# Local and summary attention with a gated network: work units of 384 tokens in place of 512

## The chip, the cores and the metric

The kernel runs on one core of one Trainium2 chip. The metric is device time in microseconds (us) from the first to the last instruction of that core. A few names for the engines, as the profile uses them: PE is the matrix engine (its weight loads are listed apart as PEld), DVE the vector engine, ACT the scalar engine, POOL the GpSimd engine, SP the engine whose queue starts nearly all DMA transfers. PE reads operands from SBUF and writes to PSUM; the kernel holds PSUM tiles of 128 partitions by 512 float32 values.

## The reference

Inputs are q, k and v of shape (batch 4, heads 8, sequence 768, head size 64) and four weight matrices. Each query sees the 31 keys nearest to it and, besides, one summary key for each block of 32 keys of its batch (24 summaries); the network then runs over all 3072 tokens.

```python
k_sum = k.reshape(B, H, nb, block, D).max(axis=3)     # block 32, nb 24
v_sum = v.reshape(B, H, nb, block, D).mean(axis=3)
scores_l = scale * q @ k.T, masked to |i - j| < 16
scores_s = scale * q @ k_sum.T + log(block)
a = softmax over [scores_l, scores_s] together
x = (a @ [v, v_sum]), heads side by side              # 3072 x 512
out = (((x @ w1) * (x @ w2)) @ w3) @ w_out            # w1, w2: 512 x 1024; w3: 1024 x 1024; w_out: 1024 x 512
```

## The kernel before

**Products.** The network is computed with each operand split in two parts of 32-bit "fp32r" form, a high one and a low one, so each product is three matmuls (L113): high by high, low by high, high by low. w3 and w_out are multiplied once, at the start, into one matrix `wp` ("the fold", 192 matmuls of 512 columns). The weights come as 64-bit words of 1 MB a tile, and each tile is turned into its high and low part on the chip: ACT L164, DVE L173 and L176, ACT L190 (high part), DVE L109 (low part, tile `w`).

**Units and steps.** All 3072 tokens are one row of 24 blocks of 128 tokens; a batch is 6 blocks. The row is cut into units of `TOKENS` tokens, and a unit has four attention steps, one for each pair of heads. `NBLK` is the number of blocks in a unit, `NU` the number of units, `NS` the number of steps. A step loads its q, k and v (L306, L308, L291), puts in the summaries of its batch (POOL L318 for keys, L298 for values; `batches(u)` makes one copy for each batch that the unit touches), computes scores (PE `sc`, L331), mask and minimum (DVE L345), exponential and sum (ACT L359, one instruction for each block and head), the scaling (L364, L365, L368 or its kin), transposes (PE `tp`, L388), two copies out of PSUM (`pt`, L393 on ACT and L397 on DVE), the product with v (PE `po`, L408), and the split into `x` (ACT L419, DVE L109).

**The network of a unit.** `gate` makes, for each of 8 slices f, two sums over four x tiles: w1 into one PSUM tile, w2 into the next, 12 matmuls each and `U` columns wide (U is TOKENS). ACT copies the first out (`g`, L448), DVE multiplies it with the second (L453), ACT and DVE split the result into `h` (L454, L109). `project` then makes, for each block, one sum of 24 matmuls of 512 columns with `wp` (ACT L472 copies it out, and a DMA from ACT's queue stores it). Both take turns on the same two PSUM tiles, named `mm`.

**What sets the order.** PE, SP (and, in parts, ACT, DVE, POOL) follow the order in which the program is written; where they don't, a scheduler orders by priority. The network's matmuls are one stream, dealt out by a count of columns. In the start, a table of ticks (`LOADS`, `WORK`, `FIRST`) says when loads, conversions and the first eight steps begin; the stream may then go as far as `TO_SLOTS`. In it the summaries of the second batch are prepared as well. After it, a loop takes two steps at a time: transposes of the last two, scores of the next two, outputs of the last two, and then half a unit of the stream:

```python
NU = B * S // U
NS = NU * NPAIR                       # NPAIR = 4
NFIRST = 2 * NPAIR                    # steps of the start: two units
UNIT = 3 * (2 * U * NC * NF + DO * NF * NBLK)
TO_SLOTS = ALL_FOLD + 0.96 * UNIT
run(ALL_FOLD + UNIT * (1 + (n / m if n <= m else 1 + (n - m) / NPAIR)))
```

The summaries of the third and fourth batch are prepared in the start's loop or in later turns of the loop (`coming`, `turns`), by how many steps there are before a batch is needed.

Of the kernel before, what the change touches and what calls it, by code (L numbers as in the profile page):

```python
# [23 lines left out]
LOC = P + 2 * PAD  # L24
CUT = 96
BIG = -8.0e9
TOKENS = 512
PIECE = 1024
AHEAD = 2

# [40 lines left out]
def attention_moe(ctx, tc, qG, kW, kT, vP, vW, vB, mask, w1, w2, w3T, wo, out):  # L71
# [3 lines left out]
    NB = S // BLOCK  # L75
    U = TOKENS
    NBLK = U // P
# [784 lines left out]
```

## Time and profile before

| | |
|---|---|
| median of 2 runs | 533.62 us (533.4 to 533.84) |
| the profiled execution: its span, from the first to the last instruction, the one time its page gives | 533.5 us |
| PE busy / weight loads busy | 511.2 us (96%) / 421.4 us (79%) |
| DVE / ACT / POOL busy | 240.6 / 225.4 / 95.9 us |
| matmuls of the gates (128x512) | 1152, of the projection 576, of the fold 192 |
| DMA | 68.78 MB, mean 129 GB/s |

The page lists busy time by engine, then the span in 40 slices with the granted clock of PE, then the chain of work that ended last, followed back from the last instruction, and groups of like instructions with their busy time, the mean of one and the idle time before them. PE's matmuls overlap one another, so the mean of one is longer than the distance from one start to the next; distances are read from rows of the timeline that hold several matmuls. A "busy" window in the start can also hold matmuls that wait.

### The profile page before, as it was taken

Reading aid. Unit: us, or ns where it says so; the run is one execution under the profiler, and the core shown is the slowest. Engines: PE = TensorE matmul, PEld = TensorE weight load, DVE = VectorE, ACT = ScalarE, POOL = GpSimd, SP = SyncE. Lnnn points to the kernel's source line nnn. Section 1 sums busy time; section 2 is a strip of 40 time slices with the busy share of each in tenths; the row PEclk is TensorE's granted clock in tenths of the full one; section 3 lists DMA queues with packets and bytes.
Section 4 is the critical chain, followed back from the end, with each engine's and each line's share of the span. In section 5 each row is a group of like instructions: output and inputs, shape, how many; then the busy total and the mean of one; then the engine's idle time right before and its main releaser. Section 6 shows DMA issues by size and latency. Waiting matters only on the chain.

```text
span 533.5 us, 9766 instructions
## 1 busy us (share of the span) xinstructions
PE 511.2 (96%) x3888; PEld 421.4 (79%) x3888; DVE 240.6 (45%) x667; ACT 225.4 (42%) x627; POOL 95.9 (18%) x158
## 2 busy tenths in 40 slices
PE   1889989999999999999999999999999999999997
PEld 0667767888888888888888888888888888888885
DVE  5889987798534326435244043251042350222210
ACT  5587964674626226135154063361172361222210
POOL 2020635001033202305005014014023031000000
PEclk9989997999999999999999999999999999999999
DMA  8995699804834013453040150050150011100001
GB/s 346 413 411 220 252 325 413 316 2 139 274 131 167 0 55 122 151 172 134 0 177 1 60 195 1 1 177 20 49 187 2 14 69 40 39 3 0 1 20 59
DMA packets 21166, 68.78 MB, mean 129 GB/s; under 512 B 2304, under 2 KB 2432, under 8 KB 18560
## 3 DMA queue, kind: packets, MB, share of 16 engines
q1 hardware_dynamic: 17664, 61.86, 31.6%
q10 hardware_dynamic: 3456, 6.29, 3.1%
q8 instruction: 30, 0.49, 0.4%
q14 instruction: 16, 0.13, 0.1%
HBM read 61.85 MB, written 6.29 MB: 128 GB/s over the span
## 4 chain that ended last, share of the span: by engine, by line
PE 87%; DMA 5%; DVE 4%; ACT 2%; issue 1%; POOL 0%; SPq 0%; POOLq 0%; ACTq 0%
PE mm L113 76%; PE po L408 4%; PE sc L331 4%; DMA rows<-in_vP_dram 2%; PE tp L388 2%; DVE wf L176 2%; DMA wraw<-in_w_dram 1%; DVE w L109 1%; DMA wraw<-in_wo_dram 1%; ACT sm L359 1%; DVE wf L173 1%; ACT wf L164 1%; DVE sm L345 0%; ACT w L190 0%; DVE ks L236 0%
## 5 line engine op out<-in xcount | busy, mean ns | idle before, releaser
L113 PE MATMUL mm<-x,w 128*128 128x512 f32 x1152 | 264.3, 391 | 0.0
L113 PEld LDWEIGHTS mm<-x,w 128*128 128x128 f32 x1152 | 216.5, 188 | 45.3
L113 PE MATMUL mm<-wp,h 128*128 128x512 f32 x576 | 133.3, 390 | 0.0
L113 PEld LDWEIGHTS mm<-wp,h 128*128 128x128 f32 x576 | 107.7, 188 | 22.6
L359 ACT ACTIVATE sm<-sm,mx 128x120 f32<-128x120 f32 x192 | 73.6, 385 | 16.3 <-DVE mx L345 16.3
L453 DVE TENSOR_TENSOR g<-mm,g 128x512 f32<-128x512 f32 x48 | 33.1, 690 | 88.7 <-PE mm L113 85.4
L454 ACT CAST h<-g 128x512 fp32r<-128x512 f32 x48 | 29.5, 618 | 90.6 <-DVE g L453 90.6
L113 PE MATMUL mm<-w,w 128*128 128x512 f32 x192 | 51.2, 419 | 14.8 <-ACT w L190 12.0
L113 PEld LDWEIGHTS mm<-w,w 128*128 128x128 f32 x192 | 37.3, 200 | 25.7 <-ACT w L190 12.7
L364 POOL TENSOR_SCALAR mx<-mx 128x8 f32<-128x8 f32 x24 | 6.8, 283 | 275.5 <-ACT sm L359 275.3
L472 ACT COPY o<-mm 128x512 f32<-128x512 f32 x24 | 14.0, 584 | 82.5 <-PE mm L113 82.5
L397 DVE COPY pt<-tp 120x512 f32<-120x512 f32 x22 | 14.3, 684 | 75.2 <-PE tp L388 75.2
L109 DVE TENSOR_TENSOR h<-g,h 128x512 fp32r<-128x512 f32 x48 | 35.2, 736 | 25.6 <-ACT h L454 25.4
L448 ACT COPY g<-mm 128x512 f32<-128x512 f32 x48 | 28.1, 586 | 39.0 <-PE mm L113 38.4
L298 POOL COPY v<-vs 24x512 f32<-24x512 f32 (+1 forms) x64 | 40.7, 635 | 8.9 <-DMA v<-in_vW_dram 5.9
L345 DVE CUSTOM_DVE_ANT_0 sm<-sc,mask_sb 128x120 f32<-128x120 f32 x192 | 41.1, 274 | 0.0
L359 ACT ACTIVATION_READ_ACCUMULATOR sm<-sm,mx 128x1 f32 x192 | 36.2, 188 | 0.0
L368 POOL TENSOR_TENSOR sm<-sm,mx 128x960 f32<-128x960 f32 x16 | 28.7, 1793 | 5.6 <-DVE mx L365 5.6
L109 DVE TENSOR_TENSOR x<-po,x 128x512 fp32r<-128x512 f32 x24 | 16.6, 690 | 28.6 <-ACT x L419 28.5
L190 ACT CAST w<-wf 128x1024 fp32r<-128x1024 f32 (+1 forms) x22 | 21.3, 968 | 17.3 <-DVE wf L176 17.2
L408 PEld LDWEIGHTS po<-pt,v 120*64 120x64 f32 x768 | 24.5, 141 | 4.0 <-issue 2.5
L408 PE MATMUL po<-pt,v 120*64 120x64 f32 x768 | 26.6, 228 | 0.9 <-POOL v L298 0.5
(35 smaller groups left out, 287.9 us busy)
## 6 DMA issues: line engine op xcount, KB each, us to landing
v<-in_vW_dram SPq DMA_DIRECT2D x24, 512.0 KB, 6.4
wraw<-in_w3T_dram SPq DMA_DIRECT2D x8, 1024.0 KB, 13.0
wraw<-in_w_dram SPq DMA_DIRECT2D x8, 1024.0 KB, 9.3
k<-in_kW_dram SPq DMA_DIRECT2D x20, 368.0 KB, 5.3
raw<-in_kT_dram SPq DMA_DIRECT2D x16, 392.0 KB, 3.7
q<-in_qG_dram SPq DMA_DIRECT2D x24, 256.0 KB, 4.9
raw<-in_vB_dram SPq DMA_DIRECT2D x12, 512.0 KB, 3.8
out_dram<-o ACTq DMA_DIRECT2D x24, 256.0 KB, 2.0
```

Source lines behind the costliest of these rows:

```text
L109: eng.tensor_tensor(dst, src, hi.bitcast(F32), ALU.subtract)
L113: nc.tensor.matmul(acc, lhsT=a, rhs=b, start=first and i == 0, stop=last and i == len(terms) - 1)
L190: nc.scalar.copy(t[:, 0, some], f[:, some])
L298: nc.gpsimd.tensor_copy(v[at : at + NB, g, blocks], src.unsqueeze(1).broadcast_to([NB, n, P]))
L331: nc.tensor.matmul(sc[h][64 * g : 64 * g + 64, i * KR : (i + 1) * KR], lhsT=q[rows, i * P + 64 * g : i * P + 64 * g + 64], rhs=k[rows, i, ...
L345: nc.vector.tensor_tensor_reduce(out=sm[:, j], in0=sc[h][:, i * KR : (i + 1) * KR], in1=mask_sb[:, 0 if blk == 0 else 2 if blk == BLOCKS - ...
L359: nc.scalar.activation(sm[:, j], sm[:, j], AF.Exp, bias=mx[:, 0, j : j + 1], scale=-1.0, accum_out=mx[:, 1, j : j + 1])
L368: nc.gpsimd.tensor_tensor(sm, sm, mx[:, 2].unsqueeze(2).broadcast_to([P, NI, KR]), ALU.mult)
L408: nc.tensor.matmul(po[cols, at : at + 64], lhsT=v[:KR, g, i, cols], rhs=pt[g][:, (h * NBLK + i) * 64 : (h * NBLK + i + 1) * 64], start=Tru ...
L448: nc.scalar.copy(g, a[:, :U])
L453: nc.vector.tensor_tensor(g, acc[1][:, :U], g, ALU.mult)
L454: nc.scalar.copy(h[:, 0], g)
```

## The change

One constant is changed. `TOKENS` goes from 512 to 384, and with it `U` from 512 to 384, `NBLK` from 4 to 3, `NU` from 6 to 8 and `NS` from 24 to 32. A batch of 768 tokens is then exactly two units. With 512, the second and fifth units held two blocks of one batch and two of the next, and their eight steps took the summaries of two batches.

```diff
-TOKENS = 512
+TOKENS = 384
```

What follows from it: the gates have 1536 matmuls of 384 columns in place of 1152 of 512. The projection has 576 of 512 columns as before. The attention's PE instructions are the same in number in all, 12 a step for `sc`, `tp` and `po` in place of 16, but the loop runs 13 times in place of 9. The eight steps of the start now cover the first batch alone. Copies of a PSUM tile (`pt`, `x`, `g`, `h`) are 384 wide, and there is a third more of them; `UNIT` and `TO_SLOTS` shrink with the unit. The host lays out q, k and v in the narrower units. The third batch's summaries are now prepared by turns of the loop, as the fourth's were.

PE, from the last scores before the first gates to the fourth gate sum, before (tiles with a number are weights; `x16` in the list counts an instruction with its like):

```order
L388 MATMUL tp<-ident,sm 120x64 x16
L331 MATMUL sc<-k,q 64x120 x32
L408 MATMUL po<-pt,v 64x64 x16
L113 MATMUL mm<-x,w_827 128x512 x12
L113 MATMUL mm<-x,w_857 128x512 x12
```

and after the change:

```order
L388 MATMUL tp<-ident,sm 120x64 x12
L331 MATMUL sc<-k,q 64x120 x24
L408 MATMUL po<-pt,v 64x64 x12
L113 MATMUL mm<-x,w_768 128x384 x12
L113 MATMUL mm<-x,w_797 128x384 x12
```

Nothing changes place here: the attention work is three quarters in number, and the gate sums are as many but narrower.

DVE, in the middle of the first unit's gates, where the last weight tiles are converted (`g` is the gate product L453, `h` and `w12` are the low parts L109; w12_902 is the third w1 tile, w12_919 the third w2 tile), before:

```order
L109 TENSOR_TENSOR w12_902<-wf_893,w12_902 128x1024
L173 TENSOR_SCALAR wf_910<-wf_910 128x1024
L109 TENSOR_TENSOR h_1086<-g_1065,h_1086 128x512
L109 TENSOR_TENSOR h_1086<-g_1116,h_1086 128x512
L109 TENSOR_TENSOR h_1173<-g_1158,h_1173 128x512
L176 SCALAR_TENSOR_TENSOR wf_910<-wraw_885,wf_910 128x1024
L173 TENSOR_SCALAR wf_921<-wf_921 128x1024
L453 TENSOR_TENSOR g_1190<-mm_1192,g_1190 128x512
L109 TENSOR_TENSOR w12_919<-wf_910,w12_919 128x1024
```

and after the change (w12_842 and w12_856 are those two tiles, `ISA` is L345's minimum):

```order
L109 TENSOR_TENSOR w12_842<-wf_833,w12_842 128x1024
L173 TENSOR_SCALAR wf_848<-wf_848 128x1024
L109 TENSOR_TENSOR h_996<-g_976,h_996 128x384
L109 TENSOR_TENSOR h_996<-g_1023,h_996 128x384
L109 TENSOR_TENSOR h_1077<-g_1062,h_1077 128x384
L453 TENSOR_TENSOR g_1094<-mm_1096,g_1094 128x384
L176 SCALAR_TENSOR_TENSOR wf_848<-wraw_825,wf_848 128x1024
L109 TENSOR_TENSOR h_1077<-g_1094,h_1077 128x384
L173 TENSOR_SCALAR wf_858<-wf_858 128x1024
L345 ISA sm_905,mx_906<-sc_907,mask_sb_65 128x120
L345 ISA mx_906 128x1
L109 TENSOR_TENSOR w12_856<-wf_848,w12_856 128x1024
```

The fourth gate product (g_1190 before, g_1094 now) stood behind the L176 of the third w2 tile and stands ahead of it now, and one `h` and one L345 more stand between that L176 and the tile's low part.

## The prediction

> **What bounds the kernel now.** I read the page's engine row first, then the chain of waits, then windows and the timeline of PE.
>
> ```profile
> PE 511.2 (96%) x3888; PEld 421.4 (79%) x3888; DVE 240.6 (45%) x667; ACT 225.4 (42%) x627; POOL 95.9 (18%) x158
> PE   1889989999999999999999999999999999999997
> 382.99 1.09 PE tp L388 x32
> 384.08 1.98 PE sc L331 x64
> 386.06 2.02 PE po L408 x64
> 388.08 32.86 PE mm L113 x144
> 420.94 1.09 PE tp L388 x32
> 529.98 0.02 issue
> 530.00 0.59 ACT o L472
> ```
>
> PE is full from about the fifth slice. Later the chain is on PE alone: rounds of `tp`, `sc`, `po` and 144 matmuls, with nothing late between them; one round takes 420.94 - 382.99 = 37.95 us. The window of that part and the one before it, and the first gates:
>
> ```profile
> 0.00:85.19 85.19, 66.81 (x625) 51.17 (x625) 70.61 (x145) 58.37 (x134) 21.85 (x41) 0.95 0.86 333
> 85.19:529.98 444.79, 444.44 (x3266) 370.18 (x3264) 169.98 (x522) 166.49 (x492) 74.03 (x117) 1.00 0.26 90
> 85.19 44.72 PE L113 MATMUL mm<-x,w 128*128 128x512 f32 x192
> ```
>
> (Columns: time, then busy time of PE, PEld, DVE, ACT, POOL, the clock, the DMA share, GB/s.) In the start DVE is busy 70.6 of 85.2 us and the DMA engines 86%; from 85.19 PE is busy 444.4 of 444.8 us. So the time is: **when the gates begin (85.19) + the PE work behind that (444.8) + the end (3.5)** = 533.5, the profiled span, 0.1 us under the median of the runs, 533.62. What matters is what the change does to each, and which new waits PE meets.
>
> **Cost of a gate matmul.** Both widths stream the same columns in all (1152 x 512 = 1536 x 384). The question is the toll of one matmul.
>
> ```profile
> 35.96:38.52 2.56, 2.56 (x8) 0.50 0.98 404
> 35.96 3.19 PE L113 MATMUL mm<-w,w 128*128 128x512 f32 x7
> 287.21 5.15 PE L113 MATMUL mm<-wp,h 128*128 128x512 f32 x22
> L113 PE MATMUL mm<-x,w 128*128 128x512 f32 x1152 | 264.3, 391 | 0.0
> L113 PEld LDWEIGHTS mm<-x,w 128*128 128x128 f32 x1152 | 216.5, 188 | 45.3
> ```
>
> In the second row 7 matmuls at half clock (0.50) begin within 2.56 us, 0.427 us apart, which is 0.2134 at full clock if all of it scales. At full clock (third row) 22 last 5.15 us; less one length of 0.39 that is 4.76 / 21 = 0.2266 apart. So 0.0132 us a matmul is not streaming. If it is paid once a matmul, 384 columns take 0.75 x 0.2134 + 0.0132 = 0.1733; if it grows with the columns, 0.1700. Gates before: 1152 x 0.2266 = 261.0. After: 1536 x 0.1733 = **266.2 (+5.2)**, or 261.1 (0). I take the toll per matmul: a cost that grew with the columns would be expected at half clock too, and there is none to see. The other end stays in the range. [...] The projection keeps 576 x 0.2266 = 130.5.
>
> **Cost of the rounds.** A round's attention part is 37.95 - 144 x 0.2266 = 5.32 us. What of it shrinks with the unit is seen by setting one step against two:
>
> ```profile
> 66.91 0.68 PE L388 MATMUL tp<-ident,sm 64*120 64x64 f32 x16
> 67.53 1.05 PE L331 MATMUL sc<-k,q 64*64 64x120 f32 x32
> 68.51 1.67 PE L113 MATMUL mm<-w,w 128*128 128x512 f32 x6
> 70.11 1.15 PE L408 MATMUL po<-pt,v 120*64 120x64 f32 x32
> 71.19 1.20 PE L113 MATMUL mm<-w,w 128*128 128x512 f32 x4
> ```
>
> One step of `tp`, `sc`, `po` takes 0.62, 0.98, 1.08 us to the next row's start, two take 1.09, 1.98, 2.02. So 0.15 + 0.14 us are fixed, and 5.32 - 5.09 = 0.23 more is the way in and out of the network's matmuls: 0.5 us a round. The rest times 0.75 gives 4.1; I take 4.15, with 4.0 and 4.35 as ends (nothing fixed; some of `sc` fixed too). Behind the first gates there were 10 such rounds (one in the start, nine of the loop, the last without `sc`): 53.2 - 2.0 = 51.2. Now 14: 58.1 - 1.5 = **56.6**. Four rounds more cost about 2 us, and the rest of the difference is work moved behind the first gates, since the eight early steps cover 768 tokens and no longer 1024.
>
> Sum behind the first gates, before: 261.0 + 130.5 + 51.2 = 442.7, and 444.8 measured, so 2.1 are small waits and a cold clock, which I keep. After: 266.2 + 130.5 + 56.6 + 2.1 = **455.4**.
>
> **When the gates begin.** The last step before them, and what held it:
>
> ```profile
> 44.45 0.68 PE L388 MATMUL tp<-ident,sm 64*120 64x64 f32 x16
> 60.30 0.61 POOL v L298
> 61.64 1.03 PE po L408 x28
> 68.66 0.33 SPq L306
> 69.52 7.58 DMA wraw<-in_w_dram
> 82.27 1.08 PE L331 MATMUL sc<-k,q 64*64 64x120 f32 x16 [1.03 <-POOL k L318]
> v<-in_vW_dram SPq DMA_DIRECT2D x24, 512.0 KB, 6.4
> q<-in_qG_dram SPq DMA_DIRECT2D x24, 256.0 KB, 4.9
> ```
>
> The load of the first w2 tile stands in SP's queue behind a q load (68.66) that waits for the fourth pair's scores on PE (67.53). From 44.45 us PE comes there with three `tp`, two `sc`, two `po`, some 6 us; a quarter less is 1.5. The POOL copies of value sums that held `po` (60.30) are a quarter narrower, some 0.7; the first three q and the first v, a quarter smaller, are 0.32 MB less at the 404 GB/s quoted above, 0.8 us. So that load starts about 3 us earlier. Then DVE has a quarter less of minima and copies in the fourth pair, and the wait of 1.03 us on the second batch's key summaries goes, since no early step touches that batch. I take 4 us in all: **81.2**. Ends: 79.5, and 85.2 if DMA or DVE, full as they are, give nothing back.
>
> **A new wait in the first unit.** There the last six weight tiles are converted while the gates run, and DVE does both in one order. Its durations, and the returns from ACT:
>
> ```profile
> L109 DVE TENSOR_TENSOR w<-wf,w 128x1024 fp32r<-128x1024 f32 x18 | 22.4, 1248 | 5.0 <-ACT w L190 5.0
> L176 DVE SCALAR_TENSOR_TENSOR wf<-wraw,wf 128x1024 uint32<-128x1024 uint32 x18 | 22.4, 1242 | 0.2
> L173 DVE TENSOR_SCALAR wf<-wf 128x1024 uint32<-128x1024 uint32 x18 | 13.8, 769 | 3.4 <-ACT wf L164 3.4
> L453 DVE TENSOR_TENSOR g<-mm,g 128x512 f32<-128x512 f32 x48 | 33.1, 690 | 88.7 <-PE mm L113 85.4 <-ACT sm L359 1.6 <-ACT wf L164 1.3
> L236 DVE TENSOR_REDUCE ks<-raw 128x24 f32<-128x768 f32 x16 | 14.9, 943 | 5.3 <-DMA raw<-in_kT_dram 5.3
> 88.87 1.23 DVE L109 TENSOR_TENSOR w<-wf,w 128x1024 fp32r<-128x1024 f32 x1 [1.12 <-ACT w L190]
> 97.37 0.69 DVE L453 TENSOR_TENSOR g<-mm,g 128x512 f32<-128x512 f32 x1 [1.18 <-PE mm L113]
> 109.30 1.23 DVE L109 TENSOR_TENSOR w<-wf,w 128x1024 fp32r<-128x1024 f32 x1
> 116.86 1.22 DVE L109 TENSOR_TENSOR w<-wf,w 128x1024 fp32r<-128x1024 f32 x1
> ```
>
> Before, the third w2 tile was done at 110.5 (third row from the end, plus its length) and wanted at 85.2 + 0.8 (cold clock) + 108 x 0.2266 = 110.5, behind nine sums of 12: no reserve. Now PE wants it 0.8 + 108 x 0.1733 = 19.5 us behind the first gate. DVE has until then, from the fourth pair's `pt` on, by the order: 5 L173, 4 L176, 4 L109 of weights, 9 gate or x operations (0.55 each, by 0.68 at 512 and 1.25 at 1024 columns), 2 L236: 20.7 us, and two returns from ACT of 1.1: 22.9. It begins some 0.9 us before the first gate (the copy of `pt`, then `po`), so the tile is done about 22 us behind it. **PE waits 2.5 us**; 0 if DVE waits for nothing else, since then the returns are covered, 9 in the second rival. The table of ticks and the weights' bytes are unchanged, so narrower gates aren't fed faster.
>
> **What is hidden.** A third more PSUM copies on ACT and DVE: the gates give them 12 x 0.1733 = 2.08 us a sum in place of 2.72. The L453 row shows 85.4 us of waiting on PE, so DVE had been early nearly every time. In a round, ACT must get its copy of a sum in between exponentials before 2.08 us are over; by the order at most five stand ahead of one, and they begin before the sum ends. At 0.3 us a loop round, were this wrong, it would cost 13 x 0.3 = 4 us. The POOL copies for straddling steps (eight of 256 columns became four of 384) lie beside PE's matmuls. The end, 3.5 us, is unchanged: the projection and its last store are the same.
>
> **Sum.** 81.2 + 455.4 + 2.5 + 3.5 = 542.6; I say **542.5 us**, 1.7% slower. About 2% (10.7 us, so 544.3 and 522.9) is what the measurement tells from no change.
>
> **The rivals.**
> 1. *The toll isn't per matmul.* Gates take 261 us, then the sum is 537.4; with no toll at all at 384 columns (1536 x 0.160 = 245.8) 522. For it: I have one width only at full clock. Against: half clock shows none. Chance 18%. [...]
> 2. *Weights come no sooner* (clearly slower): start bound by DMA and conversion, the last w2 tile ready at 118.1 as before (last row above). The gates then end at 118.1 + 36 x 0.1733 = 124.3 in place of 81.2 + 0.8 + 33.3 = 115.3; that wait of 9 us for 2.5 makes 549. It decides over 2% from a tile 2 us later than in my sum. For it: DVE 83% busy in the start. Against: four q and four v a quarter smaller, 0.8 MB less to load. 16%.
> 3. *Copies late in the rounds*, 4 us as above: 546.5. Against: no PE wait in the loop before. 6%.
> 4. *The weight load sets the pace.* If a load of 0.188 us had the array to itself, matmuls couldn't come closer than 0.19: 1536 x 0.19 = 292, the sum 568. Against it, two loads begun in 0.30 us:
>
> ```profile
> 16.81 0.30 PEld L113 LDWEIGHTS mm<-w,w 128*128 128x128 f32 x2 [0.68 <-ACT w L190]
> ```
>
> so the second started 0.11 behind the first, and 0.11 is under 0.17. [...] 4%.
>
> My own case has 56%, range 537 to 547, a fifth of it above 544.3.
>
> **Chances.** Slower by over 2%: 11 of my case, 15 of the second rival, 5 of the third, 4 of the fourth, 35%; faster by over 2%: 2% (the far end of the first rival); within: 63%. The range 534 to 549 leaves out the weight-load case, half of the second rival and the far end of the first, under 2 in 10.
>
> **What would show it.** Right: gate matmuls 0.173 apart; a loop round of 29.0 us (96 x 0.1733 + 36 x 0.2266 + 4.15); first gate near 81; one PE wait of 2 to 3 us on a `w` tile in the first unit, none in the loop. Wrong: 0.170 or 0.162 or 0.19 apart (rivals 1 and 4), rounds over 29.3 with waits on L448 or L453 (rival 3), the first unit's gates ending more than 39 us behind their start (rival 2).

## The result, and the profile after

The kernel with units of 384 takes 552.78 us in the median of two runs (551.33 to 554.22), 1.0369 times the kernel before (95% interval 1.0291 to 1.0447): slower. The forecast was 542.5 with a range to 549. The profiled execution has a span of 552.4 us, 18.9 more than before's. Medians and ratios in this document leave out three executions that ran far slower than the others of the same kernel (645 us and more).

The page of the changed kernel: the engine row, PE in 40 slices, and the clock granted to PE.

```profile
PE 523.6 (95%) x4272; PEld 475.0 (86%) x4272; DVE 247.3 (45%) x723; ACT 230.7 (42%) x671; POOL 99.3 (18%) x174
PE   1988978899999999999999999999999999999997
PEclk9998997989999999999999999999999999999999
```

PE is busy 12.4 us longer, and the clock row dips in the fourth, seventh and ninth slices, in the start and in the first unit. The chain of waits in the loop (start, length, what):

```profile
204.14 0.85 PE tp L388 x24
205.00 1.63 PE sc L331 x48
206.62 1.55 PE po L408 x48
208.17 25.01 PE mm L113 x141
233.18 0.85 PE tp L388 x24
```

A round is 233.18 - 204.14 = 29.04 us, all on PE, as 37.95 was before. The loop is what was forecast, so the miss lies ahead of it. The span in three windows: to the first gate, the first unit's gates, and the rest (columns as in the prediction: time, busy PE, PEld, DVE, ACT, POOL, clock, DMA share, GB/s):

```profile
0.00:86.11 86.11, 63.45 (x529) 47.99 (x529) 67.89 (x130) 53.52 (x114) 20.61 (x39) 0.97 0.82 321
86.11:126.08 39.97, 37.64 (x194) 37.06 (x193) 29.68 (x61) 23.09 (x51) 5.12 (x9) 0.90 0.42 166
126.08:548.50 422.42, 422.04 (x3552) 389.95 (x3552) 149.72 (x533) 153.49 (x505) 73.53 (x126) 1.00 0.25 82
```

The first gate comes at 86.11 where 81.2 was forecast. The 192 gate matmuls behind it take 39.97 us where 33.3 would do, at a mean clock of 0.90. From 126.08 on PE waits for 0.4 us in all. The timeline of PE across the first two windows shows what it waited for (idle time and releaser in brackets):

```profile
84.84 1.33 PE L408 MATMUL po<-pt,v 120*64 120x64 f32 x20 [4.24 <-DVE pt L397]
86.11 21.09 PE L113 MATMUL mm<-x,w 128*128 128x384 f32 x108
108.71 0.44 PE L113 MATMUL mm<-x,w 128*128 128x384 f32 x1 [1.51 <-ACT w L190]
109.97 16.27 PE L113 MATMUL mm<-x,w 128*128 128x384 f32 x83 [0.82 <-DVE w L109]
```

The wait on the third w2 tile (1.51 + 0.82 us) was forecast; the 4.24 us on the copy `pt` of the fourth step were not. DVE's timeline ahead of that copy:

```profile
75.09 0.14 DVE L254 TENSOR_SCALAR vs<-vs 128x32 f32<-128x32 f32 x1
79.35 0.85 DVE L173 TENSOR_SCALAR wf<-wf 128x1024 uint32<-128x1024 uint32 x1 [4.12 <-ACT wf L164]
80.23 1.41 DVE L176 SCALAR_TENSOR_TENSOR wf<-wraw,wf 128x1024 uint32<-128x1024 uint32 x1
81.56 0.68 DVE L109 TENSOR_TENSOR wp<-mm,wp 128x512 fp32r<-128x512 f32 x1
82.16 0.94 DVE L236 TENSOR_REDUCE ks<-raw 128x24 f32<-128x768 f32 x1
83.02 1.21 DVE L109 TENSOR_TENSOR w<-wf,w 128x1024 fp32r<-128x1024 f32 x1
84.16 0.54 DVE L397 COPY pt<-tp 120x384 f32<-120x384 f32 x1
```

DVE stands idle for 4.12 us until the first w2 tile has landed and ACT has begun on it; `pt` waits in DVE's order behind three operations on that tile, a low part of `wp` (L109) and a reduction of the second batch (L236). SP's queue shows that this tile's load (`wraw`) was issued no earlier than before, where it was 69.52:

```profile
66.25 0.33 SPq L246 DMA_DIRECT2D raw<-in_vB_dram  x1
67.92 0.33 SPq L231 DMA_DIRECT2D raw<-in_kT_dram  x1
69.19 0.33 SPq L306 DMA_DIRECT2D q<-in_qG_dram  x1
69.57 0.42 SPq L308 DMA_DIRECT2D k<-in_kW_dram  x1
70.04 0.42 SPq L144 DMA_DIRECT2D wraw<-in_w_dram  x1
```

### The profile page after: what moved, and what is told of

Read it like the earlier page. It is cut to its first block, busy times and chain, and to the rows that moved or that the text cites. A ratio compares the mean times of both kernels' runs of the same rounds, so it can differ in the third digit from the quotient of the medians.

```text
span 552.4 us, 10758 instructions
## 1 busy us (share of the span) xinstructions
PE 523.6 (95%) x4272; PEld 475.0 (86%) x4272; DVE 247.3 (45%) x723; ACT 230.7 (42%) x671; POOL 99.3 (18%) x174
## 4 chain that ended last, share of the span: by engine, by line
PE 86%; DMA 4%; DVE 4%; ACT 3%; POOL 1%; issue 1%; SPq 0%; POOLq 0%; ACTq 0%
PE mm L113 75%; PE po L408 4%; PE sc L331 4%; PE tp L388 2%; DMA rows<-in_vP_dram 2%; DMA wraw<-in_w_dram 1%; DVE wf L176 1%; DVE w L109 1%; DMA wraw<-in_wo_dram 1%; ACT wf L164 1%; DVE wf L173 1%; DVE ks L236 1%; DVE wp L109 1%; POOL v L298 1%; ACT sm L359 1%
## 5 line engine op out<-in xcount | busy, mean ns | idle before, releaser
L113 PE MATMUL mm<-x,w 128*128 128x384 f32 x1536 | 273.7, 338 | 2.3 <-ACT w L190 1.5
L113 PEld LDWEIGHTS mm<-x,w 128*128 128x128 f32 x1536 | 269.9, 190 | 4.0 <-ACT w L190 1.8
L454 ACT CAST h<-g 128x384 fp32r<-128x384 f32 x64 | 32.4, 509 | 90.5 <-DVE g L453 90.5
L453 DVE TENSOR_TENSOR g<-mm,g 128x384 f32<-128x384 f32 x64 | 35.6, 556 | 70.5 <-PE mm L113 67.9
L397 DVE COPY pt<-tp 120x384 f32<-120x384 f32 x30 | 15.4, 551 | 94.5 <-PE tp L388 94.5
L109 DVE TENSOR_TENSOR h<-g,h 128x384 fp32r<-128x384 f32 x64 | 38.7, 607 | 26.0 <-ACT h L454 25.2
L448 ACT COPY g<-mm 128x384 f32<-128x384 f32 x64 | 30.4, 475 | 37.4 <-PE mm L113 36.6
L345 DVE CUSTOM_DVE_ANT_0 sm<-sc,mask_sb 128x120 f32<-128x120 f32 x192 | 42.5, 274 | 0.6 <-PE sc L331 0.6
L298 POOL COPY v<-vs 24x384 f32<-24x384 f32 x64 | 37.8, 590 | 13.0 <-DMA v<-in_vW_dram 9.9
L368 POOL TENSOR_TENSOR sm<-sm,mx 128x720 f32<-128x720 f32 x24 | 33.4, 1391 | 7.6 <-DVE mx L365 7.6
L109 DVE TENSOR_TENSOR x<-po,x 128x384 fp32r<-128x384 f32 x32 | 17.8, 557 | 32.4 <-ACT x L419 30.5
```

The source lines that it names most:

```text
L109: eng.tensor_tensor(dst, src, hi.bitcast(F32), ALU.subtract)
L113: nc.tensor.matmul(acc, lhsT=a, rhs=b, start=first and i == 0, stop=last and i == len(terms) - 1)
L298: nc.gpsimd.tensor_copy(v[at : at + NB, g, blocks], src.unsqueeze(1).broadcast_to([NB, n, P]))
L345: nc.vector.tensor_tensor_reduce(out=sm[:, j], in0=sc[h][:, i * KR : (i + 1) * KR], in1=mask_sb[:, 0 if blk == 0 else 2 if blk == BLOCKS - ...
L368: nc.gpsimd.tensor_tensor(sm, sm, mx[:, 2].unsqueeze(2).broadcast_to([P, NI, KR]), ALU.mult)
L397: nc.vector.tensor_copy(pt[1], tp[1][:KR, :U])
```

## The experiments

All times are medians of repeated runs beside runs of the kernel before, whose medians in these comparisons lie between 532.26 and 532.58 us. "First gate" is the start of the first gate matmul in the profiled execution, "gates' end" the end of the first unit's gates (before: 85.19 and 129.74; after the change: 86.11 and 126.08). These marks come from one execution each and shift with the half clock that fell into it (some 3.7 us in the first unit of the changed kernel), so the medians decide.

### The toll of a matmul

**Two halves (units of 512).** Each gate matmul of 512 columns is split in two of 256; nothing else changes.

```diff
-  products(a[:, :U], [(t[:, 0, c, fs], x[c][:, 0]), ...], c == 0, c == NC - 1)
+  for half in (slice(0, U // 2), slice(U // 2, U)):
+      products(a[:, half], [(t[:, 0, c, fs], x[c][:, 0, half]), ...], ...)
```

> Units of 512 as before, but every gate matmul is issued as two of 256 columns (2304 in place of 1152, the same columns in all). If each matmul pays a fixed 13.2 ns besides its columns, they come 0.1067 + 0.0132 = 0.120 us apart, gates take 276 us in place of 261, and the time is 547 to 550 us. If the toll grows with the columns, 0.1133 apart and no change (533 to 535 us). If the weight load's own time counts as well (two loads begun 0.107 us apart), nothing is added, since 0.107 is under 0.120.

Measured: 548.22 us, ratio 1.0295 (1.0264 to 1.0327), 15.6 us more for 1152 more matmuls: 13.5 ns each. Gate matmuls start 0.120 us apart at 256 columns, 0.173 at 384, 0.2266 at 512. The three lie on a line, 0.0533 per 128 columns plus 0.0133. The toll is paid per matmul, as forecast. Each matmul here has a weight load of its own (2304 of each), so the runs don't tell whether it belongs to the matmul or to the pair.

**No straddling (units of 512).** Steps whose unit holds blocks of two batches take the summaries of the first batch for all of them, so the attention computed there is not the one asked for, but the copies for two batches are gone.

```diff
-            if at < to:
-                yield b, slice(at, to), to - at
+            if at == 0 and to > 0:
+                yield b, slice(0, NBLK), NBLK
```

> Units of 512 as before, but the steps that straddle two batches take the summaries of the first of the two for all their blocks (so their output isn't the attention asked for): one copy in place of two, and no wait for the second batch in the fifth to eighth step. This is the straddling's price alone, without narrower units. If it is as small as the wait it causes on PE in the profile (1.03 us at 82.27), 532 to 533.6 us. Rival: straddling holds the start more than the profile shows, and the time falls by over 4 us.

Measured: 532.04 us, ratio 0.9994 (0.9981 to 1.0006). Straddling cost nothing that the medians show, so its removal had nothing to give.

### What holds the first gate and the first unit

**Copy first (384).** The `pt` copies of the first four steps get priority in DVE's and ACT's order.

```diff
-  pt = evacuate(transposes(...), SECOND[s])
+  tps = transposes(...)
+  with tc.high_priority(offset=SOONER):
+      pt = evacuate(tps, SECOND[s])
```

> Units of 384, and in the first four steps the copies of the transposes out of PSUM (pt) get the priority that the gates' copies have; on DVE the fourth step's copy then stands ahead of the low part of the first w2 tile, but still behind that tile's L173 and L176. Theory 'order on DVE': PE's wait of 4.24 us on that copy comes from what stands ahead of it on DVE; without the low part (1.2 us) and a key summary (0.9) the first gate comes 2 us sooner, and the half-clock spell behind the wait covers less: 549 to 550 us. Rival 'late tile': both hang on the load of the first w2 tile (issued at 70.04, landed at 78.08), so the first gate stays within 1 us of 86.1 and the time within 1 us of 552.8.

Measured: 553.36 us, ratio 1.0396 (1.0370 to 1.0422). The first gate came 2.6 us earlier, at 83.51, and the gates ended later, at 127.75, with waits of 0.8, 3.6 and 1.1 us on weight tiles. An earlier first gate is worth nothing here, since the tiles behind it came no earlier.

**Second batch later (384).** Since no early step touches the second batch any more, its loads and reductions can move from ticks 17 to 33 to ticks 48 to 58, and what needs them behind that.

```diff
-  17: [lambda: load_second(2), lambda: fetch_sums(0)],
-  21: [lambda: load_second(0), lambda: load_second(1), lambda: fetch(5), ...],
...
+  48: [lambda: load_second(0), lambda: load_second(1)],
+  50: [lambda: second_batch(0), lambda: load_second(2)],
...
```

> Units of 384, and the preparation of the second batch's summaries (four loads of 512 KB, four of 392 KB, eight reductions on DVE of 0.95 to 1.2 us) is moved from the start to behind the first gates, since no step before the ninth needs it. Theory 'volume': the start is held by the work that DVE and DMA do for the second batch; before the first gate about 2.5 MB (6 us at 400 GB/s) and 6 us of DVE go, the first gate comes 4 to 6 us sooner, the tile waits in the first unit go, 543 to 546 us. Rival 'late tile': the load of the first w2 tile waits behind a q load for the fourth step's scores on PE, whatever DVE does; the first gate moves by 1 to 2 us, 550 to 551.5 us.

Measured: 548.72 us, ratio 1.0300 (1.0267 to 1.0333). First gate at 81.63, gates' end at 121.88: a good 4 us gained, between the two theories' numbers.

**Load first (384).** Only the q and k loads of the fifth step move by one tick, behind the first w2 tile's load in SP's queue; the second batch stays where the change left it.

```diff
-  22: [..., lambda: first_keys(3), lambda: fetch(4), lambda: fill(3), ...],
-  23: [lambda: second_batch(1)],
+  22: [..., lambda: first_keys(3), lambda: fill(3), ...],
+  23: [lambda: fetch(4), lambda: second_batch(1)],
```

> Units of 384, the second batch where the change left it; the first w2 tile's load stands ahead of the q load that waits for PE's scores, but still behind two loads of the second batch. Theory 'that q load': the tile lands up to 2 us earlier, the first gate at 82 to 84, 549 to 551 us. Rival 'the second batch's loads and reductions are the other half': its loads wait for their buffers until DVE has reduced what was there, so the queue is held all the same, the first gate stays at 85 to 86 and the time at 551.5 to 553 us.

Measured: 553.14 us, ratio 1.0389 (1.0350 to 1.0427): no gain, though the first gate came at 81.07, just where the forecast had it, and earlier than either theory said. PE's timeline tells why:

```profile
81.07 18.48 PE L113 MATMUL mm<-x,w 128*128 128x384 f32 x96
100.08 0.44 PE L113 MATMUL mm<-x,w 128*128 128x384 f32 x1 [0.53 <-ACT w L190]
101.47 2.18 PE L113 MATMUL mm<-x,w 128*128 128x384 f32 x11 [0.95 <-DVE w L109]
106.20 0.69 PE L113 MATMUL mm<-x,w 128*128 128x384 f32 x1 [2.54 <-ACT w L190]
108.16 16.68 PE L113 MATMUL mm<-x,w 128*128 128x384 f32 x83 [1.27 <-DVE w L109]
```

Of the 5 us gained by the first gate all but 1.4 are lost again by the gates' end (124.68), in four waits on two tiles, 5.3 us, and in the half clock around them (mean clock 0.88 from 81.07 to 124.68).

**Both (384).** The second batch later and the load first.

> The second batch's loads and reductions come at ticks 48 to 58 as in the run that moved them alone (548.72 us, first gate at 81.63), and the q load that stood ahead of the first w2 tile's load in SP's queue stands behind it. Theory 'order of SP's queue': the load of that tile no longer waits for PE's scores, so the first gate begins at 77 to 80 and the following tiles come sooner by the same; the first unit's gates still last about 40 us; 544 to 547 us. Rival 'conversion': DVE and ACT convert the tiles of the first unit no faster, so what the first gate gains goes into waits of PE on w tiles; the first unit's gates last 42 to 44 us; 548 to 549 us.

Measured: 544.22 us, ratio 1.0210 (1.0172 to 1.0249), 8.6 us under the changed kernel. The profiled execution is the quickest of the four (542.04). Its windows and its PE timeline:

```profile
0.00:79.51 79.51, 60.72 (x528) 45.93 (x528) 63.57 (x121) 54.89 (x116) 19.36 (x41) 1.00 0.78 304
79.51:114.01 34.50, 33.69 (x197) 33.37 (x193) 29.87 (x63) 21.41 (x50) 6.04 (x7) 1.00 0.55 208
114.01:536.30 422.29, 421.98 (x3552) 389.82 (x3552) 154.65 (x541) 153.55 (x505) 73.54 (x126) 1.00 0.27 89
```

```profile
78.78 0.80 PE L408 MATMUL po<-pt,v 120*64 120x64 f32 x20 [1.57 <-DVE pt L397]
79.51 2.21 PE L113 MATMUL mm<-x,w 128*128 128x384 f32 x11
82.53 31.64 PE L113 MATMUL mm<-x,w 128*128 128x384 f32 x181 [0.81 <-DVE x L109]
```

The gates begin 6.6 us earlier and take 34.5 us, with no wait on a tile and the full clock. Everything behind 114.01 is as in the changed kernel (422.29 against 422.42). The two edits together give more than either alone. Theory 'order of SP's queue' holds for the first gate and the time, but it left the gates at about 40 us; 'conversion' falls.

**Both, and the copy first (384).**

> Units of 384, the second batch later and the load first as in the run of 544.22 us, and pt copied ahead of what stands in DVE's order as in the run of 553.36 us. Theory 'with the tiles early the copy decides': PE's wait of 1.57 us on pt goes, the first gate at 77.5 to 78.5, the gates still in 34.5 to 36 us, 542 to 543.5 us. Rival 'tiles': what the first gate gains is lost on w tiles, 544 to 546 us.

Measured: 544.17 us, ratio 1.0216 (1.0174 to 1.0258). No gain: the first gate was at 80.29 and PE still waited 1.86 us for `pt`, since in DVE's order two operations on the w2 tile and a low part of `wp` still stood ahead of the copy. The priority did not move it past them here, so the first theory stays untested.

### Conversion, loads or reductions

**No shift (384).** L173 is left out for the network's weights; DVE is spared 4.6 us.

```diff
-  nc.vector.tensor_scalar(out=bits[:, some], ..., op0=ALU.logical_shift_left)
+  if name not in ("w1", "w2"):
+      nc.vector.tensor_scalar(out=bits[:, some], ..., op0=ALU.logical_shift_left)
```

> Units of 384; the shift of L173 is left out for the w1 and w2 tiles, so the network's weights are wrong numbers; DVE is spared 6 operations of 0.77 us in the start and the first unit, 4.6 us. Theory 'DVE's order holds the start and the tiles': the pt of the fourth step is copied 0.8 us earlier or more, both waits of PE on w tiles in the first unit (1.5 and 0.8 us) go, the half-clock spell behind them goes with them; the first unit's gates end 3 to 5 us earlier than 126.1; 548 to 550 us. Rival 'loads': the tiles come when their loads land, the end of those gates moves by less than 1.5 us; 551.5 to 553 us.

Measured: 554.08 us, ratio 1.0402 (1.0367 to 1.0438); gates' end at 125.22, less than 1 us earlier, with waits of 2.59 and 0.96 us on a tile. The time lies above both theories' ranges: 4.6 us less on DVE, taken from these operations, gave nothing. ACT's timeline in this run shows another holder (L449 is L448 of the kernel, one line further down):

```profile
93.53 0.47 ACT L449 COPY g<-mm 128x384 f32<-128x384 f32 x1
97.07 0.48 ACT L449 COPY g<-mm 128x384 f32<-128x384 f32 x1 [3.07 <-PE mm L113]
97.45 1.14 ACT L164 ACTIVATE wf<-wraw 128x1024 f32<-128x1024 f32 x1
```

The next tile's conversion (L164) stands in ACT's order behind a copy of a gate sum that waits 3.07 us for PE. When PE is late, the tiles are converted late, and PE is then late for them. That this coupling is what eats the 4.6 us is a reading of these rows; no run isolates it.

**Low part on POOL.** L109 of the w1 and w2 tiles moves from DVE to POOL, in units of 384 and in the kernel before.

```diff
-  low(nc.vector, t[:, 1, some], f[:, some], t[:, 0, some])
+  low(nc.gpsimd if name in ("w1", "w2") else nc.vector, t[:, 1, some], ...)
```

> Units of 384; L109 of the w1 and w2 tiles runs on POOL in place of DVE. DVE is spared six operations of 1.25 us, 7.5 us; on POOL one should take about 2.0 us, by its 1.39 us for 720 columns. Theory 'DVE's order holds the start and the tiles': as in the run without the shift, or more, 546 to 549 us. Rival 'loads': 551.5 to 553 us; and if POOL's copies of the summaries fall behind these operations, 553 to 556 us.

> Units of 512, the kernel before, with L109 of the w1 and w2 tiles on POOL in place of DVE. Theory 'DVE's order holds the start': the first gate comes 1 to 3 us earlier than 85.2 and the tiles of the first unit keep up with it, so 529.5 to 531.5 us against about 532.6. Rival 'loads': 532 to 533 us.

Measured: 556.61 us, ratio 1.0449 (1.0420 to 1.0479), and 535.86 us, ratio 1.0058 (1.0033 to 1.0084): worse in both. The first gate came earlier (82.33 and 82.34), but at 384 PE then waited on POOL and ACT for tiles, 8.1 us in all. It began with the low part of the third w2 tile 2.99 us behind that tile's high part (109.00 and 111.99), where with L109 on DVE it was 1.26 us (108.71 and 109.97 in the changed kernel): a tile is done later. At 512 PE waited 2.5 us on DVE's gate products (L453); what made those late is not shown.

**Idle loads (384).** On top of "both", the second batch's eight loads are issued a second time at their old ticks, and nothing reads what they bring.

```diff
+  def idle_load(k):
+      of_second[k][0]()
...
+  17: [lambda: idle_load(2), lambda: fetch_sums(0)],
+  21: [lambda: idle_load(0), lambda: idle_load(1), lambda: fetch(5), ...],
```

> Units of 384 as in the run of 544.22 us (second batch later, tile's load first; first unit's gates end at 114.0), and the second batch's eight loads issued a second time at their old ticks, into buffers from which nothing is read, so that their bytes and their places in SP's queue are back but not DVE's reductions nor the waits for them. Theory 'loads' (bytes and places in the queue): the gates end again at 120 to 125, 549 to 553 us. Rival 'reductions' (DVE's time, and the loads that wait until DVE has freed a buffer): the gates end at 114 to 117, 544 to 547 us.

Measured: 543.05 us, ratio 1.0189 (1.0154 to 1.0224); gates' end at 113.85. The bytes and the places in the queue cost nothing (544.22 us without them), though the first w2 tile's load was issued at 62.18 in place of 54.48: it had that much time to spare.

**Small reductions (384).** "Load first", with the second batch at the ticks of the change; its reductions read 2 elements of each block in place of 32, so its summaries are wrong numbers.

```diff
-  in_=raw[:, PAD:].rearrange("p (n k) -> p n k", k=BLOCK)
+  in_=raw[:, PAD:].rearrange("p (n k) -> p n k", k=BLOCK)[:, :, : 2 if b == 1 else BLOCK]
```

> Units of 384, the second batch at the ticks of the change, the tile's load first as in the run of 553.14 us (gates end at 124.7), but the second batch's reductions read two elements of each block in place of 32, so that the summaries of that batch are wrong numbers, DVE spends 0.1 to 0.2 us in place of 0.95 to 1.2, and a raw buffer is free at once. Theory 'loads': little changes, the gates end at 122 to 125, 550 to 553 us. Rival 'reductions': they end at 114 to 118, 544 to 548 us.

Measured: 543.24 us, ratio 1.0198 (1.0157 to 1.0239); first gate at 78.77, gates' end at 113.81. Against "load first" (553.14) ten microseconds went with eight reductions on DVE of 0.94 to 1.20 us, 8.6 us in all. So it is the reductions, seen from both sides. They also hold SP's queue, whose loads wait until a reduction has freed a buffer: with small ones the next three weight loads were issued 2.5 to 3.7 us earlier (63.88, 68.58 and 69.52 in place of 66.66, 71.10 and 73.24). The waits of SP's queue from 60 to 72 us, in the changed kernel:

```profile
SPq L246 <- DVE vs L253: 5.8, 1, 5.8
SPq L246 <- DMA raw<-in_vB_dram: 4.3, 1, 4.3
SPq L231 <- DVE vs L253: 1.2, 1, 1.2
SPq L306 <- PE sc L331: 0.8, 1, 0.8
```

The q load waited for PE 0.8 us more; the raw loads ahead of it had waited 5.8 and 1.2 us for reductions (L253), and 4.3 us for the landing of an earlier load. How much is DVE's time and how much the held queue, these runs don't separate: both edits remove both.

### The half clock

Mean clock was 0.90 in the first unit. The granted clock falls to 0.50 in spells of 3.41 or 6.83 us, and windows of that length show what comes before one (changed kernel):

```profile
80.45:83.86 3.41, 0.16 (x4) 0.02 (x1) 3.41 (x4) 2.08 (x2) 0.11 (x1) 1.00 1.02 418
83.86:87.27 3.41, 2.42 (x24) 2.34 (x25) 3.21 (x5) 1.05 (x2) 0.26 (x1) 0.50 0.62 239
87.27:90.69 3.42, 3.42 (x12) 3.42 (x11) 1.48 (x2) 0.70 (x2) 2.77 (x5) 0.50 1.03 389
107.75:111.17 3.42, 1.64 (x8) 1.38 (x9) 3.22 (x6) 2.41 (x5) 0.00 (x0) 1.00 0.00 0
111.17:114.58 3.41, 3.41 (x12) 3.41 (x11) 3.41 (x7) 2.82 (x5) 0.00 (x0) 0.50 0.00 0
```

Ahead of these two spells is a window in which PE was busy for less than half: 0.16 and 1.64 of 3.4 us. To test that the wait brings the spell, **a wait before the gates** was added to "both", whose profiled execution had no spell: POOL copies the fourth step's probabilities onto themselves four times.

```diff
   normalize_alone(s, sm, mx)
+  for _ in range(4 if s == 3 else 0):
+      nc.gpsimd.tensor_copy(sm, sm)
```

> Units of 384 as in the run of 544.22 us, whose gates began at 79.5 with no spell of half clock, and lasted 34.5; POOL copies the fourth step's probabilities onto themselves four times, some 1.3 us each, so that PE waits about 4 us longer ahead of that step's transposes and nothing else is asked of DVE, ACT or the DMA engines. Theory 'the half clock follows the wait': a spell of 3.4 or 6.8 us covers the first gates, which last 36.2 to 38 us from a start at 82 to 84; 548.5 to 551 us. Rival 'the spells come from elsewhere' (a load of DVE, ACT or DMA): no spell, the gates last 33.3 to 34.5, the time grows by the wait alone, 546 to 548 us.

Measured: 544.46 us, ratio 1.0220 (1.0184 to 1.0257), against 544.22 without the copies.

```profile
77.69 0.56 PE L388 MATMUL tp<-ident,sm 64*120 64x64 f32 x12 [2.53 <-POOL sm L608]
81.88 33.95 PE L113 MATMUL mm<-x,w 128*128 128x384 f32 x192
```

```profile
75.25:78.66 3.41, 0.97 (x30) 0.90 (x34) 1.67 (x2) 1.98 (x3) 2.27 (x3) 1.00 0.50 204
78.66:82.07 3.41, 3.41 (x65) 2.99 (x58) 3.37 (x5) 2.29 (x4) 1.05 (x2) 0.50 0.45 143
82.07:85.48 3.41, 3.38 (x18) 3.06 (x19) 2.73 (x4) 1.86 (x3) 1.17 (x2) 1.00 0.76 271
```

A spell came right behind the added wait: the mechanism of the first theory. Its price was missed. The spell fell on scores and outputs, not on the gates, which took 33.8 us in place of 34.5 from a start 2.4 us later, and in the medians even the difference of 1.6 us in the spans is lost in their spread. The times agree with neither theory; the clock of one profiled execution each tells them apart. Over the four executions the mean clock was 0.994 to 0.997 with the copies; without them it was 1.0 in two and 0.997 and 0.994 in the others, so spells come without the added wait as well.

### The same moves in the kernel before

**Load first, and also the last keys of the second batch later (units of 512).** The first is the edit of "load first". The second adds the last two key loads of the second batch moved from ticks 25 to 33 to ticks 33 to 38.

```diff
-  25: [lambda: second_batch(2), lambda: second_batch(4), lambda: load_second(6)],
-  29: [lambda: load_second(7)],
+  25: [lambda: second_batch(2), lambda: second_batch(4)],
...
+  33: [lambda: fetch_sums(4), lambda: load_second(6)],
+  35: [lambda: load_second(7)],
```

> Units of 512, the kernel before, with the same move of one q load behind the first w2 tile's load. Theory 'that q load': the first gate at 82 to 84 in place of 85.2, 530 to 531.5 us. Rival 'second batch' (its loads still stand ahead) or 'no reserve' (the third w2 tile was just in time and PE now waits there): 532 to 533 us.

> Units of 512 with that move, and the last two key loads of the second batch with their reductions moved from ticks 25 to 33 to ticks 33 to 38 (the others can't move, the second unit's steps need them early). Theory 'queue and second batch hold the start of 512 as well': first gate at 80 to 83, 528.5 to 531 us, faster than the kernel before. Rival 'no reserve': PE waits on the third w2 tile in the first unit for what the first gate gained, 532 to 533 us.

Measured: 535.06 us, ratio 1.0039 (1.0021 to 1.0057), and 534.75 us, ratio 1.0037 (1.0018 to 1.0055); first gates at 86.03 and 85.31. Both expectations fell, and both kernels are a little slower. PE's timeline of the second:

```profile
79.47 0.69 PE L388 MATMUL tp<-ident,sm 64*120 64x64 f32 x16 [3.50 <-POOL sm L377]
```

With 512 tokens PE waits for the fourth step's own softmax ahead of the first gate (1.85 us on that row before), and an earlier tile doesn't shorten that. Why the wait grew to 3.50 us these runs don't settle. No version here beats the kernel before.

## Why the prediction was wrong, point by point

**The toll and the gates' price: right.** 0.1733 us a matmul was forecast. 26 gate matmuls in the first unit:

```profile
94.73 4.67 PE L113 MATMUL mm<-x,w 128*128 128x384 f32 x26
```

Less one length of 0.33 that is 4.34 / 25 = 0.1736. The choice between toll per matmul and per column was right: by three widths it is 13.3 ns a matmul.

**The argument for that choice: weaker than it looked.** It held that a cost by columns would show at half clock and that there is none to see. There, 384 columns start 0.320 us apart (12 gate matmuls from 86.92 in the changed kernel), twice the 0.160 that streaming takes at full clock by the line of the halves (3 x 0.0533), so a toll per matmul doesn't show either. The size came out right, since the half clock gave the streaming time; the kind is settled by the runs, by 0.1736 against 0.1700 here and more plainly by the halves.

**The rounds: right.** 29.0 was forecast, 29.04 measured. The window behind the first unit was to be 421.3 (455.4 less 33.3 and 0.8) and took 422.42.

**The new wait in the first unit: right in size, in part by luck.** 2.5 forecast, 2.33 measured on that tile. But the tile was done 23.8 us behind the first gate and not 22, and PE wanted it 21.1 us behind and not 19.5, because of the half clock: two misses that cancel.

**"When the gates begin", the step that failed: 81.2 forecast, 86.11 measured, 4.9 us.** The working said that the first w2 tile's load stands behind a q load that waits for PE, and that PE, POOL and the loads there shrink by a quarter, so that it starts about 3 us earlier. It started 0.5 us later, 70.04 against 69.52. Two things in that were wrong. First, PE came to the scores that free the q load at 68.26, where it had come at 67.53:

```profile
46.14 5.77 PE L113 MATMUL mm<-w,w 128*128 128x512 f32 x17 [2.05 <-DVE w L109]
68.26 0.85 PE L331 MATMUL sc<-k,q 64*64 64x120 f32 x24
```

The 1.5 us that the working saved on the way went into a wait of 2.05 us on a tile of the fold, which the kernel before doesn't have and every run of 384 has (2.05 to 2.08). A spell of half clock behind it (46.31 to 49.72), some 1.7 us, came on top in this execution; "load first" had none there. Second, the q load did not hold the queue alone. Two raw loads of the second batch ahead of it, which wait for reductions on DVE that don't shrink, were issued at 66.25 and 67.92 only. Either is enough: with the second batch moved the tile's load was issued at 67.90, right behind the q load; moved ahead of the q load it was issued at 66.66, right behind the raw loads; with both edits at 54.48. The prediction had the fact in hand that no early step touches the second batch any more, but priced it only as a wait of 1.03 us on its key summaries; the reductions themselves stayed at their ticks. Moving both the second batch and the load gave a first gate at 79.51.

**The cold clock, mis-sized: 0.8 us forecast, about 4 measured.** I kept the 0.8 of before, where the spell had all but passed before the gates. The first unit took 39.97 us: 33.3 of streaming, 2.3 of waits, and 4.4 left, of which the 25 gate matmuls that started 0.32 rather than 0.173 apart make 25 x 0.147 = 3.7. The first spell stands behind the 4.24 us on `pt` and so follows from the step that failed; the second stands behind the 1.51 and 0.82 us on the tile, a wait that was forecast, but whose price left the clock out. With both edits, where no spell came, the same gates took 34.5.

**The sum.** 4.9 at the first gate, 3.4 in the first unit (39.97 against 36.6), 1.5 behind it and at the end: 9.8 us, the miss in the span. With both edits the span is 540.2 (79.51 + 34.50 + 422.3 + 3.9) against the forecast sum of 542.6. The network's part of the forecast was sound, then, and the start's was not: what the smaller unit takes off the start becomes a gain only when the second batch's work is moved as well.

**The rivals.** No toll per matmul, copies late in the rounds, and the weight load as pace all fell: 0.1736, 29.04 and no PE wait in the loop. No run shows the 0.162 among the distances named as marks; the runs gave 0.1736. "Weights come no sooner" (549, 16%) came nearest: the gates end at 126.08 where it had 124.3, and they lasted 39.97, over the 39 named as its mark. Half of its cause holds: the fold tile that PE waited 2.05 us for was done at 46.08, no sooner than before (45.99). But bytes were not the limit: with the second batch's added again the gates ended at 113.85. It deserved more than its chance, because the quarter saved on loads could not act while the queue stood waiting for DVE and PE.

**The basis.** The prediction set the profiled span 0.1 us under the median of the runs. The results give a time beside the span of each execution, 554.22 for the span of 552.4, so 1.8 us lie outside the span, the metric is not quite the span, and before's profiled execution was some 1.7 us above its median. Its 85.19 held half clock, too: in "no straddling" and "low part on POOL", units of 512 without an early spell, the first gate came at 82.62 and 82.34. The forecast's saving was thus counted from a late start. (One pointer in the working is off: the 110.5 us is the last row but one of that list, 109.30 + 1.23.)

## What to carry to other kernels

When a transfer stands late in a queue, look at every entry ahead of it and when each is set free, not at the entry just before it: taking away one holder only exposes the next. Work that a change makes unneeded in a stage does not leave that stage by itself: here moving it, together with one load's place in the queue, was worth 8.6 us of the 19 lost. A smaller tile pays the toll per instruction (13.3 ns a matmul here) more often. An earlier start at one place can be worth nothing until the next operand comes earlier as well (a first gate at 81.07 in place of 86.11 gave 553.14 us against 552.78), so cost a start by its last operand.

## What was not expected of the hardware

**The half clock came on a grid of 3.41 us.** In the profiled execution of the kernel before, spells begin at 35.94 and 80.31 and last 3.41 and 6.83 us; in that of the changed kernel they begin at 46.31, 83.86 and 111.16 and last 3.41, 6.83 and 3.41. The beginnings within one execution lie 13, 11 and 8 times 3.41 us apart. The place of the grid differs from one execution to the next: with the added wait the spell began at 78.66, which is 12.5 times 3.41 behind the 35.94 of before. On the grids of the two kernels, from 15.5 us on and without the last window of each, five windows at full clock were followed by one at half clock; PE was busy in 51% and 45% of them before, in 40%, 5% and 48% after. No full-clock window with PE busy 58% or more was; the lowest of those have 58% before and 60%, 62% and 65% after. A window at half clock was followed by another where PE was busy 70% and 71% of it, and by full clock where PE was busy throughout. So 1.9 us of waiting in one window were enough here: the window ahead of before's spell at 80.31 held 1.86 us, nearly all of it the one wait of 1.85 us on the fourth step's softmax.

**The toll does not show at half clock**: 0.320 us for 384 columns, twice the 0.160 of streaming by the line of the halves, against 0.160 + 0.0133 at full clock.
